# Softmax exponentials a step later, and the turned matrices in another TensorE order, in an attention-and-experts kernel

## The chip, the cores and the metric

The kernel runs on one core of one Trainium2 chip. The metric is the device time of one execution in microseconds (us), as the median of three runs. The core has five engines that run their own instruction queues in order: TensorE (PE in the profile; its weight loads have a row of their own, PEld), VectorE (DVE), ScalarE (ACT), GpSimd (POOL) and SyncE (SP). [...]

## The reference

Attention over a sliding window of 64 positions, for 8 batches, 8 heads, 576 positions and head size 64, and then a layer of 8 experts with one expert chosen for each token:

```python
scores = scale * np.matmul(q, k.transpose(0, 1, 3, 2))
mask = (rel >= 0) & (rel < window)          # window = 64
scores = np.where(mask, scores, -1e9)
attn = np.exp(scores - scores.max(-1)); attn = attn / (attn.sum(-1) + 1e-9)
x = (attn @ v)                              # -> 4608 tokens of 512 numbers
logits = normed(x) @ normed(expert_emb).T / tau
expert_idx = argmax(logits); gate_w = softmax(logits)[expert_idx]
out[mask] = gate_w[mask] * (np.maximum(x[mask] @ w1[e], 0) @ w2[e])   # for each expert e
```

All inputs are float32. `w1` is 512 by 1024 and `w2` 1024 by 512 for each expert.

## The kernel before

The kernel has two parts. The **attention part** works through 36 tiles of 128 tokens (all heads of two blocks of 64 positions). `stages(s)` is one step of a software pipeline, called for s = 0 to 34; in step s different tiles are at different stages of their work. The order of the instructions is written out by hand: each engine executes its own instructions in the order in which the calls stand in `stages`. The **expert part** then splits weights and activations into a high and a low half and multiplies them on TensorE; its first pieces are mixed with the end of the attention.

One tile T goes through these calls. In step s = T:

- `scores` (L213, TensorE): the scores of the tile, into the one PSUM tile `score`, which has no second buffer.
- `own_scores` (L220, ScalarE) copies one half of `score` to the SBUF tile `sm`; `all_scores` (L223, VectorE) then copies the other half over it under a mask. Only after it may the next tile's `scores` write into `score`.
- `maxima` (L227, VectorE), `less_max` (L231, GpSimd) and `exponentials` (L234, ScalarE, in place in `sm`).

In step s = T + 1:

- `attn_transposes` (L243, TensorE) turns the exponentials into the PSUM tile `back`, which has no second buffer either; `attn_copy` (L253, ScalarE) and `attn_prev` (L256, VectorE) bring them to the tile `aM`, and `attn_own` (L259, GpSimd) masks one half of it in place. `attn_prev` waits for `attn_copy` of the same tile, because both write `aM`.

In step s = T + 2:

- `values_other` (L279) and `values_mine` (L293), both TensorE, multiply with the values. `values_other` reads what `attn_prev` wrote, `values_mine` what `attn_own` wrote. `values_mine` goes over u = 0 to 3: for u = 0 and 1 one product of 128 output rows for each half of the heads, for u = 2 and 3 two products of 64 rows each; in the tiles in which a batch begins all are of 64 rows. `x_out` (L317, L318, L321, VectorE) divides by the sums and writes the row of tokens x.

In step s = T + 3:

- `x_transposes` (L336, TensorE) turns x into the PSUM tile `xback`, `xT_evac` (L342, ScalarE) copies it out, `squares` (L329, ScalarE) sums squares.

Every fourth step has more: in steps 7, 11, ... 31 `logits_four` (L360, TensorE) multiplies four tiles of turned x with the expert embeddings into `xback`, `four_copy` (L364, ScalarE, tile `lT`) copies them out, `four_back` (L367, TensorE) turns them back, `four_out` (L370, ScalarE) stores them, and `choose` (L400 to L404, VectorE) picks the expert at the end of the step. Two steps later `ranks` (L421 to L425, TensorE), `rank_base` (L456, VectorE, ahead of `x_out`) and `ranks_out` (L465 to L471, VectorE, behind it) find each token's place, and `place` (L480, GpSimd) scatters one tile of tokens to memory in each step. In the even steps 14 to 28 the first weights are split as well, at the end of the step: a cast on ScalarE (L629) and a subtraction on VectorE (L630).

In each step, then, the engines' orders are these. TensorE: scores, logits of four, values_other, attn_transposes, x_transposes, four_back, ranks, values_mine. ScalarE: own_scores, four_copy, attn_copy, xT_evac, four_out, squares, the load of k (L174, issued from ScalarE's queue), exponentials, the weight cast. VectorE: all_scores, maxima, attn_prev, rank_base, x_out, ranks_out, choose, the weight subtraction. GpSimd: less_max, attn_own, place, tokens and count. From step 32 on the first tokens of the expert part are turned on VectorE (L799) and cast on ScalarE (L810, `x_hi`).

Of the kernel before, what the change touches and what calls it, by code (L numbers as in the profile page):

```python
# [27 lines left out]
NT = N // P  # L28
# [55 lines left out]
def attention_moe(ctx, tc, q, k, v, emb, tau, w1, w2, kc, kt, out):  # L84
# [83 lines left out]
    def load_q(T, engine=nc.sync):  # L168
        if T < NT:
            engine.dma_start(qT[:, T % RQ], q[T].rearrange("p (u c) -> p u c", u=4))  # L170
# [5 lines left out]
    def load_v(T):  # L176
        if T < NT:
            nc.sync.dma_start(vb[:, T % RV], v[T])

    def vblock(g):  # L180
        return vb[:, g // 2 % RV, g % 2]
# [4 lines left out]
    def scores(T):  # L186

        for z in range(2):
            if (2 * T + z) % NB == 0:
                for hp in range(2):  # L190
                    o = score[64 * z:64 * z + 64, hp].rearrange("p (u c) -> p u c", u=4)[:, :, :WIN]
                    nc.tensor.matmul(o, lhsT=ones[64 * hp:64 * hp + 64, :64],
                                     rhs=low[64 * hp:64 * hp + 64].rearrange("p (u c) -> p u c", u=4),
                                     start=True, stop=True)
        at = T % RK * KT
        for u in range(4):
            for hp, z in sides:
                pr, o = slice(64 * hp, 64 * hp + 64), score[64 * z:64 * z + 64, hp, u * P:(u + 1) * P]
                qz = qT[pr, T % RQ, u, z * WIN:(z + 1) * WIN]
                own = kT[pr, at + u * P + z * WIN:at + u * P + (z + 1) * WIN]  # L200
                if (2 * T + z) % NB == 0:
                    parts = [(o[:, WIN:], own)]
                elif z:
                    parts = [(o, kT[pr, at + u * P:at + (u + 1) * P])]
                else:
                    was = (T - 1) % RK * KT + u * P + WIN
                    if at:
                        hop = KT - WIN
                        parts = [(o, kT[pr, was:was + 2 * hop].rearrange("p (a c) -> p a c", a=2)[:, :, :WIN])]
                    else:  # L210
                        parts = [(o[:, :WIN], kT[pr, was:was + WIN]), (o[:, WIN:], own)]
                for to, keys in parts:
                    nc.tensor.matmul(to, lhsT=qz, rhs=keys, start=True, stop=True)  # L213
# [4 lines left out]
    def own_scores(T):  # L218
        sm[T] = ap.tile([P, 4, 2, WIN], F32, name="sm", bufs=3)
        nc.scalar.copy(sm[T], sv[:, :, :, 1])  # L220

    def all_scores(T):
        nc.vector.copy_predicated(sm[T], sel.unsqueeze(1).unsqueeze(1).to_broadcast([P, 4, 2, WIN]), sv[:, :, :, 0])  # L223
# [9 lines left out]
    def exponentials(T):  # L233
        nc.scalar.activation(sm[T], sm[T], AF.Exp, scale=0.125)  # L234

    pT, aM = {}, {}

    def attn_transposes(T):

        pT[T] = back.rearrange("p (u c) -> p u c", u=4)  # L240
        t = sm.pop(T).rearrange("p u h c -> p u (h c)")
        for u in range(4):
            nc.tensor.transpose(pT[T][:, u], t[:, u], ident)  # L243
# [7 lines left out]
    def attn_copy(T):  # L251
        aM[T] = ap.tile([P, 2, 4, P], F32, name="aM", bufs=2)
        nc.scalar.copy(aM[T][:, 0], pT[T])  # L253
# [25 lines left out]
                nc.tensor.matmul(px[T][hp][pz, u * (D + 1):(u + 1) * (D + 1)], lhsT=other[pr, u, pz],  # L279
                                 rhs=vblock(g - 1 + 2 * z)[pr, u], start=u == 0, stop=(g + z) % NB == 0 and u == 3)  # L280

    def values_mine(T):

        mine = aM.pop(T)[:, 0]
        g = 2 * T
        first = [(g + z) % NB == 0 for z in range(2)]
        halves_ = slice(0, 64), slice(64, P)
        for u in range(4):
            rows = halves_[:1] if first[1] else halves_ if first[0] or u > 1 else [slice(0, P)]
            for hp in range(2):  # L290
                pr = slice(64 * hp, 64 * hp + 64)
                for pz in rows:
                    nc.tensor.matmul(px[T][hp][pz, u * (D + 1):(u + 1) * (D + 1)], lhsT=mine[pr, u, pz],  # L293
                                     rhs=vblock(g)[pr, u], start=u == 0 and first[0] and pz.start == 0, stop=u == 3)
# [38 lines left out]
    def x_transposes(T, to=xback):  # L333
        pxT[T] = to.rearrange("p (u c) -> p u c", u=4)
        for c in range(4):
            nc.tensor.transpose(pxT[T][:, c], xr[T][:, c * P:(c + 1) * P], ident)  # L336
# [3 lines left out]
    def xT_evac(T):  # L340
        xT[T] = xfour[:, T % 8] if T < 28 else ap.tile([P, 4, P], F32, name="xT", bufs=2)
        nc.scalar.copy(xT[T], pxT.pop(T))  # L342
# [11 lines left out]
    def logits_four(G):  # L354

        a, b = GROUPS[G]
        for c in range(4):
            for T in range(a, b):
                j = 32 * (T - a)
                nc.tensor.matmul(plT[j:j + 32], lhsT=embT[:, c], rhs=xT[T][:, c], start=(c == 0), stop=(c == 3))  # L360

    def four_copy(G):
        turned_back[G] = ap.tile([P, P], F32, name="lT", bufs=1)
        nc.scalar.copy(turned_back[G], plT)  # L364

    def four_back(G):
        nc.tensor.transpose(plq.rearrange("p g e -> p (g e)"), turned_back.pop(G), ident)  # L367
# [165 lines left out]
    def warm(n, to=back):  # L533

        for _ in range(n):
            nc.tensor.matmul(to[:, :P], lhsT=ones, rhs=ones, start=True, stop=True)

    def stages(s):

        def there(d):  # L540
            return 0 <= s - d < NT

        def ending(d):
            return [G for G, (a, b) in enumerate(GROUPS) if b + d == s]

        def turned():
            if there(1):
                attn_transposes(s - 1)
                attn_copy(s - 1)

        scores(s)
        if s < 3:
            warm(12, side[1])
        own_scores(s)
        if s == 33:
            x_hi(0)
        four = [G for G in ending(3) if len(range(*GROUPS[G])) == 4]
        for G in four:
            logits_four(G)
            four_copy(G)  # L560
        load_q(s + RQ)
        if there(2):
            values_other(s - 2)
        load_v(s + RV - 3)
        for f in wsteps.get(s, ()):
            f()
        if s > 3:
            turned()
        if there(3):
            x_transposes(s - 3)  # L570
        for G in four:
            four_back(G)
        if s - 4 in (28, 29):
            logits(s - 4, side[(s + 1) % 2][:, :E])
        due = [G for G, (a, b) in enumerate(GROUPS) if s == (b + 5 if b - a == 4 else b + 4)]
        for G in due:
            if len(range(*GROUPS[G])) == 4:
                ranks(G)
        if there(2):
            values_mine(s - 2)  # L580
        all_scores(s)
        maxima(s)
        if s < 3:
            warm(12, side[1])
        if there(3):
            xT_evac(s - 3)
        for G in four:
            four_out(G)
        if s - 4 in (28, 29):
            nc.scalar.copy(x_rows(s - 4, s - 3)[:, 0, C_LOG:C_LOG + E], side[(s + 1) % 2][:, :E])  # L590
        less_max(s)
        if there(3):
            squares(s - 3)
        load_k(s + RK - 1, nc.scalar)
        if s > 3:
            attn_prev(s - 1)
            attn_own(s - 1)
        for G in due:
            if len(range(*GROUPS[G])) == 4:
                rank_base(G)  # L600
        if there(2):
            x_out(s - 2)
        if s in (32, 33):
            x_turned(s - 32)
        if 0 < s <= 3:
            turned()
            attn_prev(s - 1)
            attn_own(s - 1)
        for G in due:
            if len(range(*GROUPS[G])) == 2:  # L610
                ranks(G)
            ranks_out(G)
        for G, (a, b) in enumerate(GROUPS):
            for T in range(a, b):
                if s == (T + 9 if b - a == 4 else b + 4):
                    place(T)
        if s == 33:
            x_lo(0)
        for G in ending(3):
            choose(G)  # L620
            tokens(G)
            count(G)
        exponentials(s)
        if s == 33:
            x_hi(1)
            x_lo(1)
        if s in wsplit:
            c, at = wsplit[s]
            nc.scalar.copy(w1h[c][:, at], w1raw[c][:, at])  # L629
            nc.vector.tensor_tensor(out=w1l[c][:, at], in0=w1raw[c][:, at], in1=w1h[c][:, at].bitcast(F32), op=ALU.subtract)  # L630
        if 1 <= s < 7:
            blanks(s - 1)
# [175 lines left out]
    def x_hi(a):  # L808
        xh, xl, t = x_half(a)
        nc.scalar.copy(xh, t)  # L810
# [305 lines left out]
    T, G = NT - 1, len(GROUPS) - 1  # L1116
# [203 lines left out]
```

## Time and profile before

| what | value |
|---|---|
| median of 3 runs | 628.77 us (628.53 to 630.45) |
| the profiled execution | 622.73 us, span 621.0 us |
| TensorE busy | 593.6 us, 96% of the span |
| VectorE busy | 429.5 us, 69% |
| ScalarE busy | 354.7 us, 57% |
| GpSimd busy | 232.4 us, 37% |
| granted TensorE clock | 0.998 of full speed |

The profiled execution lies 6.0 us below the median of the runs. The span is the time between the first and last instruction of the profile, and 1.7 us of the execution lie around it. A row of the timeline gives the start of an instruction in us from the start of the span, its duration, its engine, its line, what it writes and reads, and in brackets how long the engine had been idle and what ended the wait. Instructions of one engine overlap a little, so the spacing of two starts is what an instruction costs its engine, and its duration is what whoever waits for it sees.

### The profile page before, as it was taken

How to read it: one execution, taken by the hardware profiler on the slowest of the kernel's cores; microseconds unless marked ns; L12 is line 12 of the kernel's file. 1: busy time of each engine (PE TensorE's matmuls, PEld its weight loads, DVE VectorE, ACT ScalarE, POOL GpSimd, SP SyncE). 2: the span in 40 equal slices, each digit the busy share in tenths (PEclk: the TensorE clock that was granted, in tenths of full speed). 3: DMA queues.
4: the chain of work that ended last, by engine and by line, in shares of the span. 5: the costliest groups of instructions: out<-in, count | busy, mean ns of one | idle time of the engine just before them, and what ended most of it. 6: DMA issues, size and time to landing. Idle time of an engine off the chain costs nothing. (4 is left out here: it accounts for less than half of the span.)

```text
span 621.0 us, 17807 instructions
## 1 busy us (share of the span) xinstructions
PE 593.6 (96%) x6836; PEld 528.8 (85%) x6836; DVE 429.5 (69%) x883; ACT 354.7 (57%) x567; POOL 232.4 (37%) x224
## 2 busy tenths in 40 slices
PE   8899988889899999999999999999999999999995
PEld 7687777778799898989988999899889998998884
DVE  2778888888888658686566775756765677657623
ACT  3566766666542447466466664645676466636533
POOL 2567878787833133213203331142122331222011
PEclk9999999999999999999999999999999999999999
DMA  8887888885535588886786897839778877775351
GB/s 270 276 228 238 298 264 267 244 253 152 202 114 204 134 275 279 241 269 243 245 283 208 265 295 257 271 132 327 249 242 246 277 267 222 245 262 196 114 168 38
DMA packets 85789, 143.75 MB, mean 231 GB/s; under 512 B 15797, under 2 KB 36021, under 8 KB 85696
## 3 DMA queue, kind: packets, MB, share of 16 engines
q1 hardware_dynamic: 74560, 112.87, 58.0%
q0 software_dynamic: 6000, 19.18, 8.1%
q10 hardware_dynamic: 5136, 10.49, 5.6%
q8 instruction: 55, 0.90, 0.6%
q14 instruction: 38, 0.31, 0.2%
HBM read 123.23 MB, written 20.05 MB: 231 GB/s over the span
## 5 line engine op out<-in xcount | busy, mean ns | idle before, releaser
L916 PE MATMUL ph<-xh,w1h 128*128 128x256 f32 x576 | 162.0, 281 | 1.3 <-DVE rk L456 1.3
L916 PE MATMUL ph<-xh,w1l 128*128 128x256 f32 x576 | 161.9, 281 | 1.0 <-DVE w1l L159 1.0
L916 PE MATMUL ph<-xl,w1h 128*128 128x256 f32 x576 | 161.4, 280 | 0.3 <-POOL xl L814 0.3
L988 POOL DMA_INDIRECT out<-o,rest x39 | 49.3, 1265 | 219.9 <-ACT o L985 206.3
L976 PE MATMUL po<-w2h,hh 128*128 128x512 f32 x312 | 122.2, 392 | 0.0
L976 PE MATMUL po<-w2h,hl 128*128 128x512 f32 x312 | 121.8, 390 | 0.0
L976 PE MATMUL po<-w2l,hh 128*128 128x512 f32 x312 | 121.6, 390 | 0.0
L930 DVE SCALAR_TENSOR_TENSOR hl<-ph,hh 128x512 fp32r<-128x512 f32 x78 | 53.4, 689 | 92.9 <-ACT hh L926 92.7
L159 DVE TENSOR_TENSOR w2l<-w2raw,w2h 128x1024 fp32r<-128x1024 f32 x80 | 94.7, 1220 | 24.3 <-ACT w2h L156 24.0
L916 PEld LDWEIGHTS ph<-xh,w1h 128*128 128x128 f32 x576 | 108.1, 188 | 2.1 <-issue 1.4
L916 PEld LDWEIGHTS ph<-xh,w1l 128*128 128x128 f32 x576 | 108.3, 188 | 1.6 <-DVE w1l L159 1.4
L916 PEld LDWEIGHTS ph<-xl,w1h 128*128 128x128 f32 x576 | 108.3, 188 | 1.4 <-POOL xl L814 0.5
L156 ACT CAST w2h<-w2raw 128x1024 fp32r<-128x1024 f32 x80 | 81.5, 1049 | 39.7 <-PE po L976 32.0
L159 DVE TENSOR_TENSOR w1l<-w1raw,w1h 128x1024 fp32r<-128x1024 f32 x76 | 89.2, 1236 | 11.0 <-ACT w1h L156 10.3
L814 POOL TENSOR_TENSOR xl<-xt,xh 128x512 fp32r<-128x512 f32 x37 | 47.8, 1293 | 100.4 <-ACT xh L810 100.4
L926 ACT ACTIVATE hh<-ph 128x512 fp32r<-128x512 f32 x78 | 46.1, 595 | 57.1 <-PE ph L916 43.4
L156 ACT CAST w1h<-w1raw 128x1024 fp32r<-128x1024 f32 x76 | 73.9, 1047 | 0.0
L976 PEld LDWEIGHTS po<-w2h,hl 128*128 128x128 f32 x312 | 58.6, 188 | 12.6
L976 PEld LDWEIGHTS po<-w2l,hh 128*128 128x128 f32 x312 | 58.6, 188 | 11.5
L976 PEld LDWEIGHTS po<-w2h,hh 128*128 128x128 f32 x312 | 58.6, 188 | 11.5
L810 ACT CAST xh<-xt 128x512 fp32r<-128x512 f32 x39 | 24.1, 620 | 54.6 <-DVE xt L799 53.9
L231 POOL TENSOR_TENSOR sm<-sm,st 128x512 f32<-128x512 f32 x36 | 37.5, 1041 | 36.1 <-DVE st L227 31.6
(208 smaller groups left out, 836.1 us busy)
## 6 DMA issues: line engine op xcount, KB each, us to landing
w2raw<-in_w SPq DMA_DIRECT2D x76, 512.0 KB
w1raw<-in_w SPq DMA_DIRECT2D x72, 512.0 KB
xb<-xs SPq DMA_DIRECT2D x156, 64.0 KB
v<-in_v SPq DMA_DIRECT2D x36, 260.0 KB
qT<-in_q SPq DMA_DIRECT2D x36, 256.0 KB
kT<-in_k ACTq DMA_DIRECT2D x32, 256.0 KB
w1raw<-in_w SPq DMA_DIRECT2D x8, 256.0 KB
w2raw<-in_w SPq DMA_DIRECT2D x8, 256.0 KB
```

Of the source, the lines that this page charges most:

```text
L156: nc.scalar.copy(hi[c], raw[c])
L159: eng.tensor_tensor(out=lo[c], in0=raw[c], in1=hi[c].bitcast(F32), op=ALU.subtract)
L231: nc.gpsimd.tensor_tensor(out=t, in0=t, in1=st.pop(T).unsqueeze(2).to_broadcast([P, 8, WIN]), op=ALU.subtract)
L810: nc.scalar.copy(xh, t)
L814: eng.tensor_tensor(out=xl, in0=t, in1=xh.bitcast(F32), op=ALU.subtract)
L916: nc.tensor.matmul(o, lhsT=ww[c][:, f * P:(f + 1) * P], rhs=xx[:, c, :n], start=(c == 0 and i == 0), stop=(c == 3 and i == 2))
L926: nc.scalar.activation(hh, ph[g, part], AF.Relu)
L930: nc.vector.scalar_tensor_tensor(out=hl, in0=ph.pop((g, part)), scalar=0.0, in1=hh.bitcast(F32), op0=ALU.max, op1=ALU.subtract)
L976: nc.tensor.matmul(po[a], lhsT=xx[:, f, at], rhs=ww[f // 2][:, f % 2], start=(f == 0 and i == 0), stop=(f == 7 and i == 2))
L988: d = nc.gpsimd.indirect_dma_start(out=out, out_offset=bass.IndirectOffsetOnAxis(ap=tok, axis=0), in_=o, in_offset=None, bounds_check=N - ...
```

## The change

The exponentials of tile s-1 are no longer issued at the end of step s-1 but in step s, behind `own_scores(s)` on ScalarE (for steps 4 to 34; step 34 also keeps its own at its end). On TensorE the order from step 4 on becomes: scores, logits of four, values_other, x_transposes, four_back, the half of values_mine with u = 0 and 1, attn_transposes, the half with u = 2 and 3, ranks. `xT_evac` moves ahead of `attn_copy` on ScalarE. No work is added or left out. VectorE and GpSimd keep their order of instructions.

```diff
-    def values_mine(T):
-
-        mine = aM.pop(T)[:, 0]
+    def values_mine(T, us=range(4)):
+
+        mine = aM[T][:, 0]
+        if 3 in us:
+            aM.pop(T)
...
-        for u in range(4):
+        for u in us:
...
         own_scores(s)
+        if s > 3:
+            exponentials(s - 1)
...
-        if s > 3:
-            turned()
         if there(3):
             x_transposes(s - 3)
+            xT_evac(s - 3)
         for G in four:
             four_back(G)
+        if s > 3:
+            values_mine(s - 2, range(2))
+            turned()
+        elif there(2):
+            values_mine(s - 2)
...
+        if s > 3:
+            values_mine(s - 2, range(2, 4))
         for G in due:
             if len(range(*GROUPS[G])) == 4:
                 ranks(G)
-        if there(2):
-            values_mine(s - 2)
         all_scores(s)
         maxima(s)
...
-        if there(3):
-            xT_evac(s - 3)
...
-        exponentials(s)
+        if s < 3 or s == NT - 2:
+            exponentials(s)
```

(`turned()` is `attn_transposes(s - 1)` and `attn_copy(s - 1)`.)

**TensorE, step 19**, a step with logits, from its scores to those of step 20. `score`, `back`, `xback`, `even` and `odd` are PSUM tiles, `sm_2109` holds the exponentials of tile 18, `aM_2133` the turned ones of tile 17, `xmore` the x of tile 16, `lT` the logits. Before:

```order
L213 MATMUL score_90<-kT_113,qT_112 64x128 x16
L360 MATMUL xback_87<-xfour_117,embT_97 32x128 x16
L279 MATMUL odd_89<-v_114,aM_2133 64x65 x16
L243 MATMUL back_86<-cs_91,sm_2109 128x128 x4
L336 MATMUL xback_87<-cs_91,xmore_116 128x128 x4
L367 MATMUL even_88<-cs_91,lT_2205 128x128
L293 MATMUL odd_89<-v_114,aM_2133 128x65 x4
L293 MATMUL odd_89<-v_114,aM_2133 64x65 x8
```

In the changed kernel (its lines stand two further down here; `sm_2108` is tile 18's, `aM_2142` tile 17's):

```order
L213 MATMUL score_90<-kT_113,qT_112 64x128 x16
L362 MATMUL xback_87<-xfour_117,embT_97 32x128 x16
L279 MATMUL odd_89<-v_114,aM_2142 64x65 x16
L338 MATMUL xback_87<-cs_91,xmore_116 128x128 x4
L369 MATMUL even_88<-cs_91,lT_2205 128x128
L295 MATMUL odd_89<-v_114,aM_2142 128x65 x4
L243 MATMUL back_86<-cs_91,sm_2108 128x128 x4
L295 MATMUL odd_89<-v_114,aM_2142 64x65 x8
```

The turning of the exponentials (L243) has moved from ahead of the turning of x to between the two halves of `values_mine`.

**ScalarE, from the end of step 16 to the start of step 18**; the cast L629 is one of the eight weight casts. `sm_1933` and `sm_2015` belong to tiles 16 and 17, `sm_2109` to tile 18. Before:

```order
L234 ACTIVATE sm_1933<-sm_1933 128x512
L629 CAST w1h1_105<-w1raw_99 128x512
L220 COPY sm_2015<-score_90 128x512
L253 COPY aM_2040<-back_86 128x512
L342 COPY xfour_117<-xback_87 128x512
L329 ACTIVATE sq_2071,xr_115<-xr_115 128x512
L174 DMA kT_113<-in_k 128x512
L234 ACTIVATE sm_2015<-sm_2015 128x512
L220 COPY sm_2109<-score_90 128x512
```

In the changed kernel (tile 16 is `sm_1932`, tile 17 `sm_2014`, tile 18 `sm_2108`):

```order
L636 CAST w1h1_105<-w1raw_99 128x512
L220 COPY sm_2014<-score_90 128x512
L234 ACTIVATE sm_1932<-sm_1932 128x512
L344 COPY xfour_117<-xback_87 128x512
L253 COPY aM_2049<-back_86 128x512
L331 ACTIVATE sq_2071,xr_115<-xr_115 128x512
L174 DMA kT_113<-in_k 128x512
L220 COPY sm_2108<-score_90 128x512
L234 ACTIVATE sm_2014<-sm_2014 128x512
```

The copy of a tile's scores (L220) now stands ahead of the exponentials of the tile before (L234), which stood ahead of it, and the cast no longer stands between them.

## Rows read from the trace of the kernel before

**Rows 1.** Busy time of each engine in stretches of the span: one with the weight splits (65 to 128.8 us), and the expert part (200 to 590 us). Columns: the stretch, its length, then for PE, PEld, DVE, ACT and POOL the busy us and the number of instructions, the granted clock, the DMA share and GB/s.

```profile
65.00:128.80 63.80, 56.46 (x1535) 47.45 (x1526) 54.44 (x128) 43.66 (x100) 49.85 (x49) 1.00 0.85 262
...
200.00:590.00 390.00, 388.96 (x2469) 352.46 (x2469) 261.09 (x448) 226.73 (x297) 97.52 (x75) 1.00 0.75 242
```

**Rows 2.** Waits between 20 and 165 us: who waited for whom, us in total, times, the longest.

```profile
ACT sm L234 <- POOL sm L231: 35.2, 30, 3.6
...
PEld back L243 <- ACT sm L234: 10.4, 22, 0.6
```

**Rows 3.** Timeline of the steps 5 and 6, neither of which has casts or logits: the work on one tile's scores.

```profile
29.22 0.59 ACT L220 COPY sm<-score 128x512 f32<-128x512 f32 x1
...
29.84 0.73 DVE L223 COPY_PREDICATED sm<-cs,score 128x512 f32<-128x512 uint32 x1 [0.36 <-ACT sm L220]
...
30.68 0.69 DVE L227 TENSOR_REDUCE st<-sm 128x8 f32<-128x512 f32 x1
...
31.51 1.04 POOL L231 TENSOR_TENSOR sm<-sm,st 128x512 f32<-128x512 f32 x1 [1.72 <-DVE st L227]
...
32.59 0.63 ACT L234 ACTIVATE sm<-sm 128x512 f32<-128x512 f32 x1 [0.65 <-POOL sm L231]
33.12 0.57 ACT L220 COPY sm<-score 128x512 f32<-128x512 f32 x1
```

**Rows 4.** ScalarE's timeline: the copies of own scores of tiles 9, 13, 17 and 21, four steps apart, the first two ahead of the casts, the last two among them.

```profile
45.70 0.57 ACT L220 COPY sm<-score 128x512 f32<-128x512 f32 x1
...
62.80 0.57 ACT L220 COPY sm<-score 128x512 f32<-128x512 f32 x1
...
80.68 0.58 ACT L220 COPY sm<-score 128x512 f32<-128x512 f32 x1
...
98.69 0.58 ACT L220 COPY sm<-score 128x512 f32<-128x512 f32 x1
```

**Rows 5.** Timeline, single links of one tile's way from the turned exponentials to x and on, from different steps. PEld rows are the weight loads of a group of matmuls; the last row ends with the stretch asked for, at 150.00, before which just the eight loads of 128 columns begin.

```profile
24.21 0.59 ACT L253 COPY aM<-back 128x512 f32<-128x512 f32 x1 [2.51 <-DMA qT<-in_q]
...
24.83 0.69 DVE L256 TENSOR_TENSOR aM<-back,cs 128x512 f32<-128x512 f32 x1 [1.52 <-ACT aM L253]
...
75.80 0.66 PE L243 MATMUL back<-cs,sm 128*128 128x128 f32 x4 [0.40 <-ACT sm L234]
76.18 0.47 PEld L336 LDWEIGHTS xback<-cs,xr 128*128 128x128 f32 x4
...
76.49 0.59 ACT L253 COPY aM<-back 128x512 f32<-128x512 f32 x1 [0.27 <-PE back L243]
...
76.82 0.92 PEld L293 LDWEIGHTS even<-v,aM 64*128 64x128 f32 x24 [0.17 <-issue]
...
87.10 0.68 DVE L256 TENSOR_TENSOR aM<-back,cs 128x512 f32<-128x512 f32 x1
...
88.13 0.69 DVE L321 TENSOR_TENSOR xr<-even,sums 128x512 f32<-128x512 f32 x1
...
88.66 0.56 PEld L279 LDWEIGHTS odd<-v,aM 64*64 64x64 f32 x32 [0.20 <-issue]
...
89.35 0.42 PEld L243 LDWEIGHTS back<-cs,sm 128*128 128x128 f32 x4
...
149.50 0.52 PEld L293 LDWEIGHTS even<-v,aM 64*128 64x128 f32 x8
```

**Rows 6.** Timeline, VectorE: `rank_base` in step 17.

```profile
83.44 0.18 DVE L456 TENSOR_TENSOR rk<-even,cs 128x32 f32<-128x32 f32 x1
```

**Rows 7.** Timeline, the pieces of steps with logits: TensorE and ScalarE in step 15, TensorE in step 19, and `four_copy` with the turning of x that waits for it in step 31.

```profile
72.50 0.42 PEld L336 LDWEIGHTS xback<-cs,xr 128*128 128x128 f32 x4 [0.18 <-ACT lT L364]
...
73.19 0.54 PEld L293 LDWEIGHTS odd<-v,aM 64*64 64x64 f32 x15 [0.17 <-issue]
...
86.61 0.87 PEld L213 LDWEIGHTS score<-kT,qT 64*64 64x64 f32 x32
...
87.65 0.81 PEld L360 LDWEIGHTS xback<-xfour,embT 128*32 128x32 f32 x32 [0.17 <-issue]
...
144.40 0.27 ACT L364 COPY lT<-xback 128x128 f32<-128x128 f32 x1
...
144.73 0.42 PEld L336 LDWEIGHTS xback<-cs,xr 128*128 128x128 f32 x4 [0.22 <-ACT lT L364]
```

**Rows 8.** Timeline, ScalarE: `squares` and the read of its sum.

```profile
31.20 0.65 ACT L329 ACTIVATE sq<-xr 128x512 bf16<-128x512 f32 x1
...
31.74 0.20 ACT L329 ACTIVATION_READ_ACCUMULATOR sq<-xr 128x1 f32 x1
```

**Rows 9.** Timeline, VectorE: the second and the third instruction of `choose` in step 15, of the same shape. GpSimd's `attn_own` runs from 75.05 to 76.32 us there.

```profile
75.71 0.65 DVE L401 TENSOR_TENSOR c<-xmore,m 128x32 f32<-128x32 f32 x1
...
76.40 0.19 DVE L402 TENSOR_TENSOR c<-c,cs 128x32 f32<-128x32 f32 x1
```

**Rows 10.** Timeline: `attn_prev` of tiles 3 and 33, and in step 33 VectorE's turning of tokens for the expert part with ScalarE's cast behind it.

```profile
27.58 0.69 DVE L256 TENSOR_TENSOR aM<-back,cs 128x512 f32<-128x512 f32 x1 [0.22 <-ACT aM L253]
...
156.62 0.88 DVE L799 STREAM_TRANSPOSE xt<-xb 128x128 f32<-128x128 f32 x4
...
157.54 0.62 ACT L810 CAST xh<-xt 128x512 fp32r<-128x512 f32 x1 [0.77 <-DVE xt L799]
...
160.25 0.68 DVE L256 TENSOR_TENSOR aM<-back,cs 128x512 f32<-128x512 f32 x1
```

## The prediction, on record before the changed kernel ran

> **What bounds the kernel now.** First the busy times by stretch: in the expert part TensorE is busy for 388.96 of 390 us [rows 1], so nothing in it can be gained or hidden there, and whatever the attention part loses or gains passes on to the end. In the attention TensorE is busy for 56.46 of 63.80 us while no other engine is busier [rows 1]; an engine with idle time that is still the busiest means a ring of waits over several engines. The waits name it: ScalarE's exponentials wait 35.2 us in 30 steps for GpSimd's subtraction, and the turning on TensorE waits for the exponentials in 22 steps [rows 2]. The timeline closes the ring: own copy at 29.22, masked copy 29.84, maxima 30.68, subtraction 31.51, exponentials 32.59, and the next tile's own copy at 33.12, because ScalarE has it queued behind the exponentials [rows 3]. 33.12 - 29.22 = 3.90 us for a plain step. `choose` and the rank rows on VectorE and the weight cast on ScalarE enter this ring, so that a group of four steps takes (62.80 - 45.70) = 17.10 us without casts and (98.69 - 80.68) = 18.01 us with them [rows 4].
>
> **What the change removes.** The own copy of tile s no longer waits for the exponentials of s-1 (nor for the cast between them), so this ring is cut. The own copy now names a wait for VectorE's masked copy of the tile before; TensorE's scores have waited for the same copy already, so it costs nothing. The load of k on ScalarE's queue stays where it was, behind `squares`; the exponentials only leave the place behind it. GpSimd, VectorE and SyncE keep their orders.
>
> **What it puts in its place.** The turning of the exponentials now stands behind the turning of x, and the turning of x of tile s-2 (in step s+1) waits for `x_out(s-2)`, which VectorE executes in step s behind `attn_prev(s-1)`, which waits for `attn_copy(s-1)`, which waits for the turning of the exponentials of s-1. That closes a new ring of one step. Its links, from starts to starts:
> - turning of the exponentials to `attn_copy` on ScalarE: 76.49 - 75.80 = 0.69 [rows 5];
> - `attn_copy` to `attn_prev` on VectorE: 24.83 - 24.21 = 0.62 [rows 5];
> - `attn_prev` to the product of `x_out`: 88.13 - 87.10 = 1.03 [rows 5];
> - the product to the turning of x: its duration 0.69 and the 0.03 that a signal takes in the first two links (0.69 - 0.66, 0.62 - 0.59), 0.72 [rows 5];
> - turning of x to the first half of the values: 76.82 - 76.18 = 0.64, the 0.17 of "issue" in it [rows 5];
> - first half to the turning of the exponentials: 0.52 for its eight loads [rows 5], and what TensorE loses between loads of 64 and of 128 rows: from values_other to the turning 89.35 - 88.66 - 0.56 = 0.13 [rows 5], of which I take 0.10. 0.62 in all.
>
> Sum: 0.69 + 0.62 + 1.03 + 0.72 + 0.64 + 0.62 = 4.32 us, against 3.90 of the old ring. Before, the turning stood ahead of that of x and of all the values, so this ring had 0.62 + 0.64 less and was hidden.
>
> By kinds of steps (steps 5 to 34, thirty):
> - 16 plain steps, those behind `choose` among them: 4.32 each, 69.1. The chain through `choose` comes close but stays hidden: product 0.61, its five instructions some 1.0 (0.2 each, as the 0.19 of [rows 9]), masked copy 0.84, maxima 0.83, subtraction 1.0 (the spacings of [rows 3]), then `attn_own`, 1.27 and a signal's some 0.2, which GpSimd has queued behind the subtraction, to the first half; with the ring's links up to the product and after it that is 8.7 us over two steps, against 2 x 4.32.
> - 7 steps behind a `rank_base`, which now stands inside the ring: its 0.18 [rows 6] overlaps, I take 0.10: 4.42 each, 30.9.
> - 3 steps with logits and no cast before (7, 11, 31). TensorE itself is the bound: turning to second half 0.42 + 0.17 = 0.59, second half to scores some 0.3 (an estimate: the 0.92 of all its loads less 0.52, overlapped), scores to logits 87.65 - 86.61 = 1.04, logits to values_other 88.66 - 87.65 = 1.01, that to the turning of x 0.69, turning of x with `four_back` to the values 73.19 - 72.50 = 0.69, then 0.62 [rows 5, 7]: 4.94, in sum 14.8.
> - 4 steps with logits behind a cast (15, 19, 23, 27). `four_copy` is now behind the exponentials on ScalarE, and the turning of x waits for it: turning to `attn_copy` 0.69, that copy 0.53, squares with its read 0.74 [rows 8], cast, own copy and exponentials 0.53 each (the spacing 33.12 - 32.59 of [rows 3], an estimate for each), `four_copy` to the turning of x 0.33, that to the values 0.69 [rows 7], then 0.62: 5.19, in sum 20.8.
> - In seven steps a batch begins and the first half is shorter, 0.2 at most (an estimate from 16 loads of 64 columns in some 0.3 each way). Another wait often takes its place; I count half: -0.7.
>
> 69.1 + 30.9 + 14.8 + 20.8 - 0.7 = 134.9 us. The start: `attn_prev(2)` stays at 24.83; values_other follows at 24.83 + 0.69 + 0.05, then turning of x 0.69, first half 0.64, turning 0.62, copy 0.69, `attn_prev(3)` 0.62: 28.83 instead of 27.58. The end: in step 34 the exponentials of tile 33 now stand behind the cast of the expert part's tokens (157.54) and own copy 34 on ScalarE. From the product of `x_out(31)`: 0.61, turning on VectorE 156.62 to 157.54 = 0.92 [rows 10], cast 0.53, own copy 0.53, exponentials 0.63 and a signal 0.07, 3.3, against 0.72 + 0.64 + 0.62 = 2.0 of the ring: +1.3. So `attn_prev(33)` comes at 28.83 + 134.9 + 1.3 = 165.0 instead of 160.25 [rows 10], 4.8 us later; the first products of the expert part wait for the x behind it, and from there TensorE is full. In the profile's own time 622.7 + 4.8 = 627.5; on the median of the runs, 628.77 + 4.8 = **633.6 us**.
>
> Groups of four give the same by another way: 2 x 4.32 + 4.42 + 4.94 = 18.0 against 17.10, and 18.25 against 18.01 with casts; 16 steps without and 14 with casts lose 4 x 0.9 + 3.5 x 0.25 = 4.5.
>
> [...] After the turning of x TensorE idles 0.17 us ahead of the values, and "issue" is all that the profile gives as the reason [rows 5]. If that is the wait for GpSimd's semaphore, the second half, which waits for nothing, pays none. [...]
>
> **Rivals.**
> 1. *Slower, as summed*: 633.6. Chance 0.52.
> 2. *Slower still.* `choose`'s second instruction took 0.65 where it met GpSimd's `attn_own` and the third, of the same shape, 0.19 behind it [rows 9]. In the new order I put it 0.2 us behind the end of `attn_own`; from there on, earlier, it is held, and the chain through `choose`, no longer hidden, gains up to 0.46 in seven groups, +3.2: 636.8. Chance 0.22. [...]
> 3. *No change.* The ring is shorter: no loss between loads (-0.10) and a first half of 0.40, overlapped by what follows (-0.12): 4.10 in 23 steps, -5.1: 628.5. Against it are the starts in the rows. Chance 0.16.
> 4. *Faster.* The new ring never closes since something in it runs ahead, and TensorE's own queue sets the pace. A plain step of its queue is scores 0.83, values_other 0.69, turning of x 0.64, first half 0.62, turning 0.59, second half 0.3: 3.67; a group of four is 3 x 3.67, 4.94 for the step with logits and some 0.4 for ranks (an estimate, eight small products), 16.35. Against 17.10 and 18.01 that is -0.8 x 4 - 1.7 x 3.5 = -9.2: 619.6. It decides once the ring is under 3.67, which takes a product of `x_out` that doesn't stand behind `attn_prev`. The idle of the turning [rows 2] speaks for it, VectorE's order against it. Chance 0.08.
>
> That the change doesn't do what it says is excluded by the two orders shown.
>
> **How the numbers follow.** The likeliest is 633.6. The range runs from 628.4, which takes rival 3 in, to 637.2, rival 2 with 0.4 for held weight subtractions; it leaves out rival 4 and the far end of rival 2. A measurement of this kernel can tell some 0.3%, 1.9 us, from no change: slower above 630.7, faster below 626.9. Rivals 1 and 2 are slower (0.74), a little of rival 3 too: slower 0.77. Same 0.15, faster 0.08.
>
> **What would show it.** Right: own copies some 4.3 apart in plain steps where they were 3.9, about 4.4 behind `choose` and ranks, about 5 across logits; the exponentials' wait for GpSimd nearly gone; new waits of the turning of x for the product of `x_out` (4.32 - 3.67, some 10 us in all) and of `attn_prev` for `attn_copy`; `choose`'s second instruction at 0.2. Wrong: plain steps under 4.1, or a turning of x that finds its product done; rival 2 if that instruction stays at 0.65.

## The result, and the profile after

The change is **slower**: 631.79 us median (630.24 to 636.63, 14 runs) against 627.97 us of the kernel before (626.55 to 630.59, 14 runs), ratio 1.0064 with a 95% interval of [1.0045, 1.0084]. That is +3.8 us where +4.8 was forecast. Run once more with the last experiments it gave 633.76 against 628.37, ratio 1.0083 [1.0060, 1.0107], +5.4 us.

The profiled execution took 632.80 us (span 630.9), 10.1 us more than that of before; the two traces overstate the difference, since that execution of before is 4 us under the lowest of its timed runs. Where the attention part's time went is read from the steps, then, and the size from the runs.

First the busy times by stretch, for the stretches of [rows 1], in the same columns:

```profile
65.00:128.80 63.80, 56.39 (x1439) 45.68 (x1432) 53.22 (x123) 42.14 (x93) 47.24 (x47) 1.00 0.83 255
200.00:590.00 390.00, 388.96 (x2493) 353.60 (x2492) 262.49 (x488) 220.90 (x291) 100.63 (x78) 1.00 0.77 247
```

The expert part is as full as before. In the attention TensorE is busy for as long, but with fewer products (1439 for 1535), and the other engines do less in the same time: fewer steps pass.

The waits of the change between 20 and 170 us (in total, times, the longest), to hold against [rows 2]:

```profile
ACT xfour L344 <- PE xback L338: 20.2, 25, 2.2
ACT aM L253 <- PE back L243: 11.1, 22, 0.7
DVE aM L256 <- ACT aM L253: 9.9, 15, 1.9
...
PEld even L295 <- issue: 5.0, 30, 0.2
PE xback L338 <- DVE xr L323: 4.7, 13, 0.4
PEld odd L295 <- issue: 4.4, 26, 0.2
```

The 35.2 us for which the exponentials waited for GpSimd are gone. In their place stand links of the new ring: `attn_copy` for the turning, `attn_prev` for `attn_copy`, the turning of x for the product of `x_out`. The 20.2 us of ScalarE, which has to copy the turned x, delay nothing in the steps where `attn_copy`, next in its queue, still waits for the turning (11.1 us in 22 times). One step of that ring, from the timeline of all engines (the bracket of `attn_prev` names ScalarE's small `four_out`, which stands right behind `attn_copy` there):

```profile
40.33 0.66 PE L243 MATMUL back<-cs,sm 128*128 128x128 f32 x4
40.91 0.32 PEld L295 LDWEIGHTS odd<-v,aM 64*64 64x64 f32 x16 [0.17 <-issue]
...
41.02 0.59 ACT L253 COPY aM<-back 128x512 f32<-128x512 f32 x1 [0.70 <-PE back L243]
41.71 0.69 DVE L256 TENSOR_TENSOR aM<-back,cs 128x512 f32<-128x512 f32 x1 [1.33 <-ACT xr L372]
...
42.75 0.69 DVE L323 TENSOR_TENSOR xr<-odd,sums 128x512 f32<-128x512 f32 x1
43.49 0.42 PEld L338 LDWEIGHTS xback<-cs,xr 128*128 128x128 f32 x4 [0.39 <-DVE xr L323]
...
44.08 0.52 PEld L295 LDWEIGHTS even<-v,aM 64*128 64x128 f32 x8 [0.17 <-issue]
...
44.67 0.42 PEld L243 LDWEIGHTS back<-cs,sm 128*128 128x128 f32 x4
```

Link by link, from turning to turning: 0.69 to `attn_copy`, 0.69 to `attn_prev`, 1.04 to the product, 0.74 to the turning of x, 0.59 to the first half of the values, 0.59 to the next turning: 4.34 us, where the prediction had 4.32. The next plain step takes 4.41, with 0.84 between the product and the turning of x.

### The profile page after: what moved, and what is told of

It reads as the page before. It is cut to its first block, busy times and chain, and to the rows that moved or that the text cites. A ratio compares the mean times of both kernels' runs of the same rounds, so it can differ in the third digit from the quotient of the medians.

```text
span 630.9 us, 17839 instructions
## 1 busy us (share of the span) xinstructions
PE 603.6 (96%) x6836; PEld 532.2 (84%) x6836; DVE 428.8 (68%) x883; ACT 357.2 (57%) x567; POOL 232.2 (37%) x224
```

## Experiments

Two causes were on the table: the **ring** through the product of `x_out`, and the **changes of shape** on TensorE (the mode-change theory of the expectations), which loses 0.17 us ahead of the loads of both halves of the values (56 times above). A third joined them, that exponentials which stand later are themselves late.

**1. The late exponentials alone**, TensorE in its old order.

```
  own_scores(s)
+ if s > 3:
+     exponentials(s - 1)
  ...
- exponentials(s)
+ if s < 3 or s == NT - 2:
+     exponentials(s)
```

> Late exponentials alone, TensorE's order as before (turned exponentials, turned x, ranks, values in one). Ring theory: the ring through the product of x and the turned x isn't closed here, since the turning of the exponentials doesn't stand behind a matmul that waits for x. What is left is scores, own copy (1.12 behind), exponentials (0.53), turning (0.68), turned x (0.39), values (0.64), next scores (0.83): 4.2 us a plain step, but nothing of choose, ranks or the casts in it; some 2 to 3 us over before in all, ratio 1.004 (1.000 to 1.008). Mode-change theory (the extra changes between 64 and 128 rows cost the time, not the order): two changes a step as before, so 0.99 to 1.000, since one wait is gone.

Measured: 630.24 us, ratio 1.0035 [1.0012, 1.0058]. In TensorE's timeline of this kernel the turning is again what waits, 0.76 us in each plain step, and all of TensorE's queue waits behind it:

```profile
42.45 0.66 PE L243 MATMUL back<-cs,sm 128*128 128x128 f32 x4 [0.77 <-ACT sm L234]
46.63 0.66 PE L243 MATMUL back<-cs,sm 128*128 128x128 f32 x4 [0.76 <-ACT sm L234]
```

4.18 us a step. So this half of the change, by itself, exchanges one ring for another, and no shape has changed.

**2. TensorE's order alone**, the exponentials at their old place.

```
- if s > 3:
-     exponentials(s - 1)
  ...
- if s < 3 or s == NT - 2:
-     exponentials(s)
+ exponentials(s)
```

> TensorE's new order alone, exponentials at the end of their step as before. Ring theory: the new ring (4.32) is there, and the old one, with choose, ranks and casts in it, too; each step takes the longer of the two and the chains between them: some 7.5 us over before, ratio 1.012 (1.008 to 1.017), clearly slower than the whole change. Mode-change theory: the same four changes a step as in the change, so the same ratio of 1.006, or 1.008 with the old wait kept.

Measured: 636.64 us, 1.0131 [1.0102, 1.0160], as the theory of the ring has it, by which both rings are there and the one that ends last counts in each step. TensorE's changes of shape are those of the change, and the ratio is half a per cent above it.

**3. and 4. More and less ahead of the turning.** All of the values ahead of the turned exponentials, and none of them.

```
# all ahead
- values_mine(s - 2, range(2))
+ values_mine(s - 2)
  turned()
  ...
- values_mine(s - 2, range(2, 4))
# none ahead
- values_mine(s - 2, range(2))
  turned()
  ...
- values_mine(s - 2, range(2, 4))
+ values_mine(s - 2)
```

> The change, but all of the values ahead of the turned exponentials instead of half. Ring theory: 0.3 more in the ring, 4.65 in a plain step; some 5 us over the change and 9 to 10 over before, ratio 1.015 (1.011 to 1.019). Mode-change theory: four changes a step as in the change, ratio 1.006.

> The change, but all of the values behind the turned exponentials: late exponentials, turned x, turned exponentials, values. Ring theory: 0.64 + 0.62 of the ring become 0.4, it is 3.5 and no longer binds; plain steps 3.7 to 3.9, some 5 to 6 us under the change and from 1 us under before to 1 over, ratio 0.998 to 1.002. Mode-change theory: two changes a step as before, the old ring cut: 0.99, clearly faster than before. A theory by which the late exponentials themselves cost the time: 1.006 as in the change.

Measured: 642.68 us, 1.0235 [1.0205, 1.0266], and 625.84 us, 0.9980 [0.9955, 1.0005]. TensorE's timeline, the turnings at both ends of a plain step, with all of the values ahead:

```profile
46.13 0.66 PE L243 MATMUL back<-cs,sm 128*128 128x128 f32 x4
50.93 0.66 PE L243 MATMUL back<-cs,sm 128*128 128x128 f32 x4
```

and the same of the kernel with none ahead:

```profile
37.67 0.60 PE L243 MATMUL back<-cs,sm 128*128 128x128 f32 x4
41.36 0.66 PE L243 MATMUL back<-cs,sm 128*128 128x128 f32 x4
...
58.04 0.66 PE L243 MATMUL back<-cs,sm 128*128 128x128 f32 x4
```

This is a dose: with the whole, half or none of the values inside the ring the step from the turning of tile 6 to that of tile 7 takes 4.74, 4.34 and 3.69 us, and the next one 4.80, 4.41 and 4.02. The first of the two changes shape four times a step, as often as the change and experiment 2, and the three lie up to 1.7% apart; so the number of changes of shape doesn't set the time. The last kernel has late exponentials and isn't slower than before, so lateness by itself isn't the cause either; it takes the work on the values out of the ring. TensorE's own queue, the 3.67 of the fourth rival, sets the pace there in the step shown and not in all: the four steps from 41.36 to 58.04 take 16.68 us, against the 16.35 of that rival and 17.10 in the kernel before [rows 4]. The whole dose was undershot: 0.0235 of 628.46 is 14.8 us, 9.4 were expected. The rest of the values takes 0.39 to 0.40 in a step for the 0.3 expected (4.74 for 4.34, 4.80 for 4.41, behind ranks 4.90 for 4.50), and nearly all of the thirty steps pay it: from `attn_prev(3)` to `attn_prev(33)` this trace has 148.6 us, 10.9 more than the 137.7 of the change (its trace less a stall of 1.1 us, see further down), where some 5 were expected.

**5. One link cut.** TensorE's turning of x reads the row of the tile before its own, in all but the last tiles; the routing is then computed from the wrong rows, and all the rest is the change.

```
- xr[T][:, c * P:(c + 1) * P]
+ xr[max(T - 1, 0) if T < NT - 4 else T][:, c * P:(c + 1) * P]
```

> The change, with the turning of x on TensorE reading the row of the tile before its own in all but the last tiles. That leaves out part of the computation (the routing is worked out from the wrong rows). TensorE's order, its shapes and its changes between loads of 64 and 128 rows stay those of the change, and so does all of VectorE, ScalarE and GpSimd; only the link from the product of x_out to the turning of x is cut. The theory of the ring: with that link cut, plain steps fall from 4.34 us to somewhere between 3.66 (TensorE's own queue) and 4.1, and the wait of the turning of x for the product is gone; what is late next is the chain through choose, masked copy, maxima, subtraction and attn_own to the first half of the values, 4.9 us in a step behind choose, so that the end comes only 1 to 3 us earlier. The theory that the change of shapes costs the time: plain steps stay at 4.3.

Measured: 629.36 us in one run. Order, shapes and their changes are untouched. TensorE's timeline of this kernel:

```profile
39.03 0.66 PE L243 MATMUL back<-cs,sm 128*128 128x128 f32 x4
...
43.06 0.66 PE L243 MATMUL back<-cs,sm 128*128 128x128 f32 x4
...
46.98 0.66 PE L295 MATMUL odd<-v,aM 64*128 64x65 f32 x8 [0.48 <-POOL aM L259]
47.57 0.66 PE L243 MATMUL back<-cs,sm 128*128 128x128 f32 x4
...
51.60 0.66 PE L243 MATMUL back<-cs,sm 128*128 128x128 f32 x4
```

The step to 43.06 takes 4.03 us where the same step of the change took 4.34, and the one to 51.60, behind ranks, 4.03 for 4.50. No turning of x waits for the product between 20 and 150 us. So the ring is there, and the product of `x_out` is a link of it.

But the step between the two, behind `choose`, takes 4.51 for 4.41: the first half of the values waits there for `attn_own`, at the end of the chain through `choose` that was expected next. In all, the loads of that half wait 5.2 us for it in 11 times between 20 and 170 us (0.9 us in the change). From `attn_prev(3)` to `attn_prev(33)` this trace has 135.5 us, the change 137.7 without its stall, and the kernel before 132.7: this one link is worth 2.2 of some 5.0 us, within the 1 to 3 expected. The rest goes only when the values leave the ring as well (132.7 in experiment 4). That order also has two changes of shape fewer in each step, so how much of the rest is the wait for `attn_own` and how much the changes of shape isn't shown.

**6. The exponentials of tile 33 early**, to test the 1.3 us that the prediction put on the end.

```
- if s > 3:
+ if s > 3 and s != NT - 2:
      exponentials(s - 1)
  ...
- if s < 3 or s == NT - 2:
+ if s < 3 or s >= NT - 3:
      exponentials(s)
```

> The change, with the exponentials of tile 33 alone at their old place, ahead of the cast of the expert part's tokens and the last own copy on ScalarE. The prediction put 1.3 us on these standing behind both. By it: attn_prev(33) comes 1.3 us earlier than in the change against attn_prev(32), TensorE's idle of 1.2 us ahead of the last turning is gone, and the time is 1.3 us under the change, ratio to the kernel before 1.003 to 1.005. If the granted clock of 0.50 that the change showed at 168 to 170 us comes from that idle, the clock stays at 1.00 here and the gain is up to 3 us, ratio 1.001 to 1.003. If the clock fell for another reason, it falls here too.

Measured: 633.18 us, 1.0079 [1.0051, 1.0107]: nothing gained. The timeline of ScalarE, TensorE and VectorE at the end, in the change:

```profile
162.41 0.69 DVE L323 TENSOR_TENSOR xr<-odd,sums 128x512 f32<-128x512 f32 x1
...
163.93 0.62 ACT L817 CAST xh<-xt 128x512 fp32r<-128x512 f32 x1 [1.46 <-DVE xt L806]
164.46 0.58 ACT L220 COPY sm<-score 128x512 f32<-128x512 f32 x1
...
165.62 0.66 PE L243 MATMUL back<-cs,sm 128*128 128x128 f32 x4 [1.21 <-ACT sm L234]
...
166.06 0.69 DVE L227 TENSOR_REDUCE st<-sm 128x8 f32<-128x512 f32 x1
...
167.00 0.69 DVE L256 TENSOR_TENSOR aM<-back,cs 128x512 f32<-128x512 f32 x1 [0.26 <-ACT aM L253]
```

and with the exponentials early:

```profile
163.51 0.69 DVE L323 TENSOR_TENSOR xr<-odd,sums 128x512 f32<-128x512 f32 x1
...
165.44 0.66 PE L243 MATMUL back<-cs,sm 128*128 128x128 f32 x4
165.56 0.58 ACT L220 COPY sm<-score 128x512 f32<-128x512 f32 x1
...
166.51 0.60 ACT L253 COPY aM<-back 128x512 f32<-128x512 f32 x1
...
167.22 0.69 DVE L227 TENSOR_REDUCE st<-sm 128x8 f32<-128x512 f32 x1
...
167.83 0.68 DVE L256 TENSOR_TENSOR aM<-back,cs 128x512 f32<-128x512 f32 x1
```

The turning does come 1.3 us earlier behind the product (1.93 us for 3.21). But `attn_prev(33)` comes only 0.27 earlier (4.32 for 4.59), since on VectorE it stands behind the maxima of tile 34, and these hang on the same cast through own copy 34. The clock stayed at 1.00 at this place, without the gain expected from that; in this execution it had fallen earlier, at 124 to 128 us. The same edit in the kernel of experiment 4 gave no more:

> The order that joins two edits: late exponentials with the turned x and the turned exponentials ahead of all of the values (plain steps 3.72 us, ratio 0.998 in its run), and the exponentials of tile 33 at their old place. If the end costs 1.3 us as the prediction has it, the time is 1.3 us under that order alone and some 2.5 us under the kernel before, ratio 0.994 to 0.997. If what stands at the end is hidden by the turning of the tokens for the expert part, the ratio stays at 0.998.

Measured: 628.22 us, 1.0010 [0.9985, 1.0036].

**7. The kernel before once more**, for a second trace.

> The kernel before once more, for a second profiled execution of it. Its first one, 622.73 us, lies 4 us under the lowest of its timed runs, so the difference of the two traces (9.9 us) is more than that of the medians (3.8 us). If the first execution was merely an early start, here the plain steps should again be 3.90 us, attn_prev(33) should come at 160 to 162, the expert part should again take all of TensorE, and the span should be 621 to 626 us. If there is something in the kernel before that comes and goes between executions (a fall of the clock at the step to the expert part, a late first own copy at 8.3 in place of 7.26), this trace may show it.

Measured: 628.72 us, span 626.9, `attn_prev(33)` at 158.72 where it came at 160.25 [rows 10]. An attention that ends 1.5 us earlier, then, and a time 6 us longer. Its windows of 2 us (columns as in [rows 1]) show why:

```profile
160.00:162.00 2.00, 1.07 (x6) 0.91 (x7) 1.97 (x3) 0.00 (x0) 2.00 (x3) 0.93 0.13 49
162.00:164.00 2.00, 2.00 (x16) 1.78 (x17) 1.84 (x3) 1.74 (x3) 1.84 (x3) 0.50 0.03 8
164.00:166.00 2.00, 2.00 (x31) 1.98 (x30) 0.00 (x0) 0.30 (x1) 1.64 (x2) 0.50 0.34 135
```

After the 1.21 us for which TensorE waits ahead of the expert part the granted clock falls to 0.50 until past 168 us, and again at 192 to 196 us, behind a wait of 1.06 us for the last counts. The first execution had the first of these waits too, 1.27 us, and no fall. The mean clock over the span is 0.988 in this trace and 0.998 in the first, and 626.9 us at the one are as much as 621.0 us at the other (an estimate, each span times its mean clock: 619.4 and 619.8 us at full clock).

**8. The two waits filled** with 32 small products of ones on TensorE, which nobody reads: in the kernel before, in the change, and in the kernel of experiment 4. The change itself ran beside them.

```
+ warm(16, xback)
  layer1(0, 0)
  ...
+ warm(16)
  sum_counts(NT)
```

> The kernel before with 32 more small products of ones on TensorE, whose results nobody reads: 16 ahead of the first products of the expert part, where TensorE idles 1.3 us at 160 to 162 us, and 16 ahead of the last sum of the counts, where it idles 1.4 us in the second trace of before. Sixty of them take 5.10 us in the start, so 16 take some 1.4 us and about fill each gap. Theory of the clock: the times of the kernel before lie between 625 and 631 us since the granted clock falls to 0.50 at these two places in most executions (mean clock 0.99 there, 0.997 in the shortest ones); with the gaps filled the mean clock rises to 0.996 or more and the median falls to 625 to 627 us, ratio 0.994 to 0.998. Rival: the clock falls for something earlier, or the products themselves delay what follows: mean clock 0.99 and ratio 1.000 to 1.003.

> The change with the same 32 products at the same two places. Theory of the clock: the attention of the change is 5.4 to 5.7 us longer, and the measured difference is only 3.8 us because its clock falls in fewer executions (mean 0.996 for 0.991). Then filling gains little here, ratio 1.003 to 1.007 to the kernel before, and against the filled kernel before the difference is 5 to 6 us. Rival, by which the clock has nothing to do with it: the difference to the filled kernel before stays at 3 to 4 us.

> The order with late exponentials and all of the values behind the turned exponentials (ratio 0.998 in its run), with the same 32 products. By the theory of the clock it gains less than the kernel before does, since its mean clock was 0.993: ratio 0.993 to 0.997, some 624 to 626 us. Rival: 0.998 to 1.001, as without them.

> The change once more, beside the other three. Expected as in its first runs: ratio 1.0045 to 1.0084, plain steps 4.34 us. By the theory of the clock, those of its executions with a mean clock of 0.997 and more lie 5 to 6 us above the executions of the kernel before with such a clock.

Measured, with the mean granted clock over the runs of each:

| kernel | median us | ratio, 95% interval | clock |
|---|---|---|---|
| before | 628.37 | | 0.992 |
| before, filled | 626.28 | 0.9975 [0.9959, 0.9991] | 0.997 |
| change | 633.76 | 1.0083 [1.0060, 1.0107] | 0.993 |
| change, filled | 634.75 | 1.0102 [1.0079, 1.0126] | 0.992 |
| experiment 4, filled | 626.74 | 0.9991 [0.9964, 1.0019] | 0.993 |

In the kernel before the filling does what the theory of the clock says: the clock rises, the median falls by 2.1 us, and the runs lie within 624.67 to 628.61. That median is close to the 626.36 of the kernel before in those of its runs that had a clock of 0.997 and more (below). It is the one version here that beats both kernels by more than its interval. TensorE's timeline of it, the fillers and the wait that is left behind them:

```profile
159.05 1.07 PE L536 MATMUL xback<-ones 128*128 128x128 bf16 x16
160.39 0.35 PE L916 MATMUL ph<-xh,w1h 128*128 128x256 f32 x1 [0.27 <-DVE rk L456]
```

In the other two it gains nothing. In the change little was expected (1.003 to 1.007), and it came out above that; in the order of experiment 4 a gain was expected, and the rival had it right. Both traces show a fall behind another wait, which no filler covers, that of the last turning for late exponentials (1.21 and 1.80 us), and further falls elsewhere, in the filled change from 25, 124, 189 and 250 us on. Windows of 2 us of the filled change, at the last turning:

```profile
166.00:168.00 2.00, 0.79 (x11) 0.53 (x13) 1.76 (x8) 1.73 (x5) 1.12 (x2) 1.00 0.52 199
168.00:170.00 2.00, 2.00 (x67) 1.91 (x70) 1.67 (x5) 1.20 (x3) 2.00 (x5) 0.69 0.37 139
170.00:172.00 2.00, 2.00 (x29) 1.82 (x22) 1.97 (x3) 0.14 (x1) 2.00 (x3) 0.50 0.00 0
```

Whether a filler ahead of the last turning would help there was not tried. Nor did it hold that the change's clock falls more rarely: its mean is 0.996 in the first runs and 0.993 in these, where the kernel before has 0.992.

## Why the prediction was right, point by point

- **What bounds the kernel, and the ring that is cut**: right. The exponentials' wait for GpSimd is gone, and with late exponentials and the values out of the new ring (experiment 4) four steps without casts take 16.68 us for the old 17.10, and four with casts 17.7 to 17.8 for 18.01 [rows 4]. Little lay behind that ring, though: from `attn_prev(3)` to `attn_prev(33)` it is 132.7 us in both. That order loses time again at the early counts, where TensorE waits 1.68 us for 0.66, and at the last turning, which waits 1.80 us for late exponentials; the rest of the account is open.
- **The ring that takes its place**: right, shown by dose (3, 4), and its link through the product by cutting it (5), which gives back 2.2 of 5.0 us. The chain through `choose` is hidden behind it, but by nothing: the prediction's own sum for it, 8.7 over two steps, is not under 2 x 4.32 = 8.64. The two steps took 8.75 in the change (40.33 to 49.08) and still 8.54 with the link cut. Plain steps take 4.34 and 4.41 for 4.32, those behind ranks 4.50 for 4.42, logits steps 4.92, 4.59 and 4.90 for 4.94, those with a cast 4.92 to 5.06 for 5.19. A group of four without casts is 17.84 (44.67 to 62.51) for 18.0, one with casts 18.17 (77.52 to 95.69) for 18.25. Of the waits of the turning of x for the product, forecast at some 10 us, 4.7 carry that name.
- **The 0.17 ahead of the values**: it comes ahead of both halves, as the sum had it: 29 of the 56 waits in the change, 0.17 us each, stand ahead of the second, though that half waits for nobody. There the term was the author's estimate, since no row of the kernel before shows such a half; why TensorE loses the 0.17, no run shows. As the whole cause of the slowdown it falls: with the same four changes of shape in a step, the step to the turning of tile 7 took 4.74 (3), 4.34 (the change) and 4.03 (5). The 0.17 ahead of the first half is a term of the ring all the same.
- **The end, +1.3 us**: the right size for the turning, for an incomplete reason. A second chain of nearly the same length, through own copy 34 and the maxima, ends at `attn_prev(33)` as well, so that the exponentials' place alone is worth 0.27 (6).
- **`attn_prev(33)` at 165.0**: it came at 167.00. From `attn_prev(3)` (28.20, forecast 28.83) that is 138.8 us for 136.2. The step that the sum missed is the early sum of counts, which lies in the tile of the turned x, `xback` (in the change):

```profile
118.00 0.66 PE L243 MATMUL back<-cs,sm 128*128 128x128 f32 x4
...
122.27 0.15 DVE L439 COPY early<-xback 128x8 f32<-128x8 f32 x1
...
122.48 0.65 PE L338 MATMUL xback<-cs,xmore 128*128 128x128 f32 x4 [1.65 <-DVE early L439]
...
123.65 0.66 PE L243 MATMUL back<-cs,sm 128*128 128x128 f32 x4
```

  In the kernel before, the same wait is 0.66 us:

```profile
117.64 0.66 PE L336 MATMUL xback<-cs,xmore 128*128 128x128 f32 x4 [0.66 <-DVE early L437]
```

  The turning of x waits until VectorE has copied those counts out, and now the turned exponentials wait with it: 5.65 us for a step of 4.3, +1.3. Another 1.1 is a stall in the step from 66.92 to 72.52 us for which the profile names only "issue", and which the second trace of the change doesn't have (4.51). Without it the 138.8 us are 137.7.
- **The size**: +4.8 forecast, +3.8 and +5.4 measured. The sum had no term for the clock, and the change's was lower in its second runs (0.993 for 0.996); for the first runs of the kernel before none is on record. Taking all runs of the two kernels with a clock on record by its mean: at 0.997 and above the kernel before has 626.36 us (median of 13) and the change 631.79 (of 6), +5.4; at 0.991 and below 628.98 (of 40) and 634.45 (of 3), +5.5. At like clock, then, the change costs 5.4 us (the lower group has only three of its runs), 0.6 over the sum, with the missed 1.3 of the counts on the same side.
- **The rivals.** The second (`choose` held by GpSimd) didn't come: that instruction took 0.19 to 0.24 us in the seven steps where it had mostly taken 0.65 [rows 9]. The 0.4 us for held weight subtractions in its range has no row behind it, and no run shows that figure: in the kernel before all eight take 0.69 us, and in the change 0.68 to 1.35, 3.3 us more in all. The seven long ones begin while `attn_own` runs on GpSimd (at 84.89 us, for one, where it runs from 84.15 to 85.43), the one of 0.68 behind its end; a group with casts still came out at 18.17 for 18.25. The third (a ring of 4.10) and the fourth (TensorE's queue at 3.67) are refuted for the change by its 4.34; experiment 4 comes near the fourth in its first steps (16.68 for 16.35) and not in those with casts.

## What to carry to other kernels

When a ring of waits is cut, add up the next ring link by link, start to start, before believing the gain: each piece of work placed between two links of a ring, here half of the values (4.34 us for 3.69), is paid in every step. Move work out of the ring, behind the link that others wait for: here that took back what the ring had cost. Expect a second chain right behind the first when one link is cut; and look for shared buffers, since whoever last read the tile is a link too (here 1.65 us for the early counts). Where medians differ by less than 1%, as here, compare executions at like granted clock: the two ends of its mean clock lie 2.6 us apart in the kernel before, 0.4%.

## What the runs showed that I had not expected

- The granted clock fell to 0.50 mostly behind waits of TensorE of 1.0 to 1.8 us, at a few places behind several shorter ones (0.31 to 0.38 us at 185 to 188 us in the filled change), and stayed there for 3 to 7 us, but not in every execution with the same waits: 1.27 us without a fall and 1.21 with one, in two executions of the kernel before. While it lasts a product of the first expert layer takes 0.41 us instead of 0.28. The medians of the kernel before at the two ends of its mean clock lie 2.6 us apart. What decides between the two wasn't settled.
- The wait for the early counts is one of these places, in the middle of the attention. It was 1.47 to 1.74 us in ten traces of the orders that turn x ahead of the exponentials, and in five of them the clock fell behind it (experiments 2, 3, 6, the filled change and the second trace of the change). TensorE's row and the windows of that second trace:

```profile
120.29 0.66 PE L338 MATMUL xback<-cs,xmore 128*128 128x128 f32 x4 [1.62 <-DVE early L439]
...
120.00:122.00 2.00, 1.71 (x14) 1.43 (x15) 1.79 (x8) 0.58 (x1) 1.05 (x1) 0.79 0.77 243
122.00:124.00 2.00, 2.00 (x36) 1.51 (x37) 0.77 (x2) 1.16 (x3) 1.46 (x2) 0.50 0.31 101
```

  The step behind it took 6.65 us there (121.69 to 128.34) and 4.51 in the first trace, at 1.00. The kernel before has 0.65 to 0.66 us of wait in its two traces and in that of its filled version, and no fall at this place.
- Products that compute nothing, in those waits, made the kernel before 2.1 us faster.
- TensorE stood still for 1.30 us in one execution of the change with no reason in the profile, at a place where the next execution has no such wait. The trace of experiment 6 has 1.31 us at the same products, that of experiment 4 0.91.
